# Rows in token order and stores on SyncE, in a retention and MLP kernel

## The chip, the cores and the metric

One core of one Trainium2 chip. The metric is device time in microseconds (us) of one launch, with all inputs and the output in HBM. Lower is better. Engines are called TensorE (PE in the profile; PEld are its weight loads), VectorE (DVE), ScalarE (ACT), GpSimd (POOL) and SyncE (SP). A name with a q behind it (ACTq, SPq) is that engine's own queue, where it issues DMAs.

## The reference

Retention over 8 batches of 576 tokens, 8 heads of 64, then a low-rank mix over tokens and an MLP over channels with a residual:

```python
def _attn_ref(q, k, v):                       # q, k, v: (8, 8, 576, 64) float32
    scores = scale * np.matmul(q, k.transpose(0, 1, 3, 2))
    gamma = 1.0 - 2.0 ** (-5.0 - np.arange(H))
    Dmat = np.where(rel >= 0, gamma[:, None, None] ** rel[None, :, :], 0.0)
    return np.matmul(scores * Dmat[None], v)

def _moe_ref(x, U, V, w_ch1, w_ch2):          # x: (8, 576, 512), U: (576, 32), V: (32, 576)
    xt = x.transpose(0, 2, 1)
    h = xt @ U @ V
    u = x + h.transpose(0, 2, 1)
    ch = np.maximum(u @ w_ch1, 0.0) @ w_ch2   # w_ch1: (512, 2048), w_ch2: (2048, 512)
    return u + ch
```

## The kernel before

A batch has four chunks of 128 tokens and 64 tokens left over; two batches share a ninth chunk, number `XC`. Each batch has a front (loads, casts, transposes, retention, mix) and two matmul stages of the MLP, which are called Y1 (relu of u times w1) and Y2 (times w2, plus u). The fronts of later batches are spread by estimated cost between the MLP steps of earlier ones, so the order of emission is the order in which each engine works.

The queries are loaded four tokens to a partition, which gives runs of 1 KB. The rows of q are then permuted within the four chunks, the permutation goes through the whole batch, and the store undoes it:

```python
SKEW, FILL1 = 0.65, (0.33, 0.85)
LOAD2, FRONT2 = (0.75, 0.12), 0.15
STQ = nc.scalar                                   # stores are issued on ACT
osb_pool = tc.tile_pool(name="osb_pool", bufs=3)
...
def load_q(g):                                    # one load, 1 KB runs
    nc.sync.dma_start(out=f, in_=q[g, :, t0:t0 + 4 * P, :].rearrange("h (p j) d -> p h j d", j=J))
...
def Y2(self, i, f0, nf=4):                        # last step of a chunk
    ...
    o_sb = osb_pool.tile([P, dm], FP32, tag="o_sb", name="o_sb")
    nc.vector.tensor_tensor(out=o_sb, in0=self.ps[i], in1=self.st["u", c], op=ALU.add)
    dst = out_flat[row0:row0 + P, :]
    if c != XC:
        dst = dst.rearrange("(p j) d -> j p d", j=J)
    stores.append(lambda: STQ.dma_start(out=dst, in_=o_sb))
    if len(stores) > 1:
        stores.pop(0)()                           # issued one chunk late
```

The loads of q, k, v and x and the transposes of six batches are issued on SyncE, the weights of the MLP on GpSimd.

## Time and profile before

| | before |
|---|---|
| median of 3 runs | 371.43 us (370.94 to 376.23) |
| profiled span | 371.7 us |
| TensorE busy | 332.2 us |
| front, to the first matmul of Y1 | 31.2 us |
| Y1 of batch 0 | 28.5 us |
| after the last matmul | 7.7 us |

The prediction shows the lines by stage and the places where TensorE stands still. One view that it lacks is that of ACT's waits. The lines give the instruction that waits, what it waited for, us in total, how many times, and the longest.

```profile
ACT y_4028 L703 <- DMA out_dram<-o_sb: 10.3, 1, 10.3
ACT s_sb L470 <- DMA out_dram<-o_sb: 7.4, 3, 4.7
...
ACT uT L388 <- DMA kT<-kv: 4.4, 1, 4.4
...
ACT y_2209 L703 <- DMA kv_f<-in_v_dram: 3.0, 1, 3.0
```

The relus (`y`) and copies (`uT`, `s_sb`) of ACT read PSUM, not a DMA's tile. 25 us of ACT's idle time end with a DMA all the same, because a store ahead of them in ACT's queue waits for one. The last two of these lines are the holes that the prediction is about; behind the 10.3 us TensorE does not stand still.

### The profile page before, as it was taken

The numbers are of one execution on the slowest core, as the hardware profiler recorded it, in microseconds if no ns is written. First come the engines' busy times: TensorE is split into PE (matmuls) and PEld (weight loads), VectorE is DVE, ScalarE is ACT, GpSimd is POOL, SyncE is SP. The second block draws the span as 40 slices with busy tenths as digits, with TensorE's granted clock in tenths as the row PEclk, the third lists the DMA queues.
The fourth block names the chain that finished last, engine by engine and source line by source line (L and its number), as shares of the span: only waits on it lengthen the run. The fifth ranks groups of instructions, "written<-read, shape, count | busy, mean of one in ns | idle before, by whom it ended". The sixth has DMA issues, their size and how long they took to land.

```text
span 371.7 us, 6390 instructions
## 1 busy us (share of the span) xinstructions
PE 332.2 (89%) x2606; PEld 184.4 (50%) x2642; DVE 154.8 (42%) x245; ACT 146.2 (39%) x284; POOL 56.2 (15%) x81
## 2 busy tenths in 40 slices
PE   3778687898997999996999999998999999999991
PEld 1454244445663554444665554545765544467540
DVE  5672546652853661463412662264424532210020
ACT  3425453135553126512574135504662156148200
POOL 8640620310130111112112001201100000000000
PEclk9989969999999999999899999999999999999997
DMA  8999899939999999988994347999902200110112
GB/s 208 194 200 243 175 176 266 203 83 180 192 173 222 167 118 178 212 131 168 159 212 91 78 110 157 218 112 159 112 15 67 56 23 0 50 65 2 56 48 64
DMA packets 127149, 49.66 MB, mean 134 GB/s; under 512 B 110192, under 2 KB 122480, under 8 KB 127120
## 3 DMA queue, kind: packets, MB, share of 16 engines
q1 hardware_dynamic: 117440, 35.48, 58.9%
q10 hardware_dynamic: 5456, 9.59, 9.1%
q0 software_dynamic: 4224, 4.19, 7.1%
q8 instruction: 20, 0.33, 0.5%
q14 instruction: 9, 0.07, 0.1%
HBM read 36.92 MB, written 9.44 MB: 125 GB/s over the span
## 4 chain that ended last, share of the span: by engine, by line
PE 67%; DMA 13%; SPq 7%; DVE 6%; ACT 3%; issue 2%; ACTq 0%; POOL 0%; DVEq 0%; POOLq 0%
DMA kv_f<-in_v_dram 5%; DMA kT<-kv 4%; PE psc L487 3%; SPq L313 3%; PE po L535 2%; DVE q_bf L299 2%; PE pu L600 2%; PE ph L581 2%; DMA q_f<-in_q_dram 2%; PE pss L465 2%; DVE ret L523 2%; SPq L401 2%; SPq L340 1%; PE psa L564 1%; DMA x_f<-in_v_dram 1%
## 5 line engine op out<-in xcount | busy, mean ns | idle before, releaser
L699 PEld LDWEIGHTS <-w_sb 128*128 128x128 bf16 x768 | 73.0, 99 | 52.7 <-issue 7.4
L303 POOL TENSOR_TENSOR kv<-kv_f,vscale 128x512 bf16<-128x512 f32 x32 | 34.3, 1071 | 190.4 <-DMA kv_f<-in_v_dram 133.6
L523 DVE TENSOR_TENSOR ret<-psc,tri 128x1024 bf16<-128x1024 f32 x32 | 39.1, 1223 | 33.0 <-PE psc L487 32.9
L470 ACT ACTIVATE s_sb<-pss 128x512 bf16<-128x512 f32 x32 | 19.1, 596 | 61.1 <-PE pss L465 36.1
L587 DVE TENSOR_TENSOR ut<-ph,xt 128x512 bf16<-128x512 f32 x36 | 24.4, 688 | 44.8 <-PE ph L581 44.8
L543 DVE TENSOR_TENSOR xt<-po,qscale 128x512 bf16<-128x512 f32 (+1 forms) x37 | 25.5, 689 | 21.1 <-PE po L535 20.9
L388 ACT ACTIVATE uT<-pu 128x512 bf16<-128x512 bf16 x32 | 18.9, 596 | 25.8 <-PE pu L600 21.3
L535 PEld LDWEIGHTS <-ret 128*128 128x128 bf16 x288 | 12.7, 100 | 10.5 <-DVE ret L523 5.9
L331 DVE CAST kv<-kv_f 128x512 bf16<-128x512 f32 x32 | 14.6, 462 | 4.2 <-DMA kv_f<-in_k_dram 4.1
L487 PE MATMUL psc<-qT,kT 64*128 64x128 bf16 x256 | 13.4, 227 | 2.9 <-DMA kT<-kv 1.7
L487 PEld LDWEIGHTS <-kT 64*128 64x128 bf16 x256 | 7.6, 97 | 15.5 <-issue 11.2
L600 PEld LDWEIGHTS <-ut 128*128 128x128 bf16 x128 | 9.6, 98 | 11.1 <-issue 3.2
L600 PE MATMUL pu<-ident,ut 128*128 128x128 bf16 x128 | 12.4, 219 | 3.0 <-ACT uT L388 2.6
L535 PE MATMUL po<-kv,ret 128*128 128x64 bf16 x256 | 13.2, 196 | 1.7 <-DVE ret L523 1.4
L299 DVE CAST q_bf<-q_f 128x512 bf16<-128x512 f32 x30 | 13.4, 509 | 3.0 <-DMA q_f<-in_q_dram 3.0
L709 PEld LDWEIGHTS <-y_4028 128*128 128x128 bf16 x80 | 7.8, 98 | 9.3
L465 PE MATMUL pss<-kv 128*128 128x128 bf16 x112 | 11.5, 229 | 0.8 <-ACT s_sb L470 0.7
L465 PEld LDWEIGHTS <-kv 128*128 128x128 bf16 x112 | 8.8, 102 | 5.9 <-issue 1.0
L410 PE MATMUL psq<-ident,q_bf 128*128 128x128 bf16 x32 | 4.1, 308 | 7.7 <-DVE q_bf L299 7.6
L709 PEld LDWEIGHTS <-y_1084 128*128 128x128 bf16 x80 | 7.2, 98 | 6.7
L709 PEld LDWEIGHTS <-y_3202 128*128 128x128 bf16 x80 | 7.2, 98 | 6.6
L709 PEld LDWEIGHTS <-y_2209 128*128 128x128 bf16 x80 | 7.2, 98 | 6.6
(585 smaller groups left out, 590.4 us busy)
## 6 DMA issues: line engine op xcount, KB each, us to landing
out_dram<-o_sb ACTq DMA_DIRECT2D x36, 256.0 KB
q_f<-in_q_dram SPq DMA_DIRECT2D x8, 1024.0 KB
kv_f<-in_k_dram SPq DMA_DIRECT2D x32, 256.0 KB
kv_f<-in_v_dram SPq DMA_DIRECT2D x32, 256.0 KB
w_sb<-in_moe_w_ch_dram POOLq DMA_DIRECT2D x8, 512.0 KB, 8.3
x_f<-in_k_dram SPq DMA_DIRECT2D x8, 128.0 KB
x_f<-in_q_dram SPq DMA_DIRECT2D x8, 128.0 KB
x_f<-in_v_dram SPq DMA_DIRECT2D x8, 128.0 KB
```

The costliest lines, as they stand in the source:

```text
L299: nc.vector.tensor_copy(out=dst, in_=src)
L303: nc.gpsimd.tensor_tensor(out=dst[rows], in0=src[rows], in1=vscale[rows, c, :, None].to_broadcast([n, H, D]), op=ALU.mult,)
L465: nc.tensor.matmul(pss[:, hp, :], pair_cols(st["k", c], hp), pair_cols(vt, hp), start=(first and hp == 0), stop=True, skip_group_check=True,)
L470: nc.scalar.activation(out=s_sb, in_=pss, func=AF.Copy)
L487: nc.tensor.matmul(psc[0:n, hl, hp, 0:n], kT[pb:pb + HALF, hp, 0:n], qTv[pb:pb + HALF, hp, 0:n], start=True, stop=True,)
L523: nc.vector.tensor_tensor(out=ret[0:n].rearrange("p (hp hl) i -> p hl hp i", hl=2)[:, :, :, 0:n], in0=psc[0:n, :, :, 0:n], in1=mask[0:n, N ...
L535: nc.tensor.matmul(po[0:n, hl, hp * D:(hp + 1) * D], ret[:, h, 0:n], vt[:, h, :], start=((c == 0 or not cross) and hp == 0), stop=True, sk ...
L543: nc.vector.tensor_tensor(out=st["x", c][rows].rearrange("p (hp hl d) -> p hl hp d", hl=2, d=D), in0=po[rows, :, 0:NHP * D].rearrange("p h ...
L587: nc.vector.tensor_tensor(out=ut, in0=ph, in1=st["x", c], op=ALU.add)
L600: nc.tensor.transpose(pu[:, cc, :], self.st["u", c][:, cc * P:(cc + 1) * P], ident)
L699: nc.tensor.matmul(ps[:, 0:n], w1_sb[:, cc, f * P:(f + 1) * P], uT[:, cc, t0:t0 + n], start=(cc == 0), stop=(cc == NCC - 1),)
L709: nc.tensor.matmul(self.ps[i], self.y1[:, f, i * P:(i + 1) * P], w2_sb[:, f, :], start=(f == 0), stop=(f == NF - 1),)
```

## The change

The intent is to have each store as one transfer of 128 natural rows, to take the stores out of ACT's queue, and to shorten the first two stages. For batches 0 and 1 q keeps its 1 KB runs, and q^T is put back in order as it leaves PSUM; the other six batches load q in natural rows of 256 B. The masks, scales and the mixer's weights need no permuted copies any more. The order of the second stage is new too.

```diff
-    SKEW = 0.65
-    FILL1 = (0.33, 0.85)
-    LOAD2 = (0.75, 0.12)
-    FRONT2 = 0.15
+    SKEW = 0.7
+    FILL1 = (0.2, 0.8)
+    LOAD2 = 0.62
+    CAST2 = (0.85, 0.3)
+    FRONT2 = 0.3
-    STQ = nc.scalar
+    STQ = nc.sync
... (one table of positions instead of two, mixer weights copied without a permutation, parts of the first casts on ACT)
     def load_q(g):
+        if g < 2:
+            return nc.sync.dma_start(... "h (p j) d -> p h j d" ...)
+        for m in range(4):
+            i = nc.sync.dma_start(
+                out=f[:, m * dm:(m + 1) * dm].rearrange("p (h d) -> p h d", d=D),
+                in_=q[g, :, t0 + m * P:t0 + (m + 1) * P, :].rearrange("h s d -> s h d"),
+            )
... (TQ)
                 self.copy(
-                    qT[:, :, h0:h0 + 2].rearrange("p m hp (j i) -> p m (hp j) i", j=J),
-                    ps.rearrange("p hp j (m i) -> p m (hp j) i", m=4),
+                    qT[:, :, hp].rearrange("p m (i j) -> p m i j", j=J),
+                    ps.rearrange("p j (m i) -> p m i j", m=4),
... (Y2)
-            if c != XC:
-                dst = dst.rearrange("(p j) d -> j p d", j=J)
... (second stage: q(1) is cast ahead of k and x, the mixer's copies come first)
-        lo2 = [(0, f) for f, in loads_of(2)]
-        spread(lo2, at(0, LOAD2[0]), at(1, LOAD2[1]))
+        def load_2():                       # all loads of batch 2 in one block
+            i = load_q(2)
+            tc.add_manual_dep(i.ins, w2_part.ins.name, SYNC)
+            for m in range(4):
+                load_kv(2, m)
+            load_x(1)
+        events.append((at(0, LOAD2), load_2))
+        spread([(0, f) for f in cast_2], at(0, CAST2[0]), at(1, CAST2[1]))
```

More of the change, by code (lines that the diff above doesn't have):

```diff
@@ L73 @@
     J = 4
-    PJ = P // J
     XC = 4
@@ L116 @@
     ident = consts.tile([P, P], BF16, name="ident")
-    perm = consts.tile([P, P], BF16, name="perm")
     tri = consts.tile([P, P], BF16, name="tri")
     trix = consts.tile([P, P], BF16, name="trix")
-    posk = consts.tile([P, NCH, H], FP32, name="posk")
-    posq = consts.tile([P, NCH, H], FP32, name="posq")
+    pos = consts.tile([P, NCH, H], FP32, name="pos")
     qscale = consts.tile([P, NCH, H], FP32, name="qscale")
@@ L150, in early_consts @@
         make_identity(nc, ident)
-        nc.vector.tensor_copy(
-            out=perm.rearrange("t (j p) -> t j p", j=J),
-            in_=ident.rearrange("t (p j) -> t j p", j=J),
-        )
         nc.gpsimd.memset(lnb, math.log(scale))
-        for t in (posk, posq):
-            iota(t[:, XC, :], [[0, H]], 4 * P, 1)
-            iota(t[HALF:P, XC, :], [[0, H]], -HALF, 1)
-        iota(posk[:, 0:4, :], [[P, 4], [0, H]], 0, 1)
-        iota(posk[:, 5:9, :], [[P, 4], [0, H]], 0, 1)
-        for j in range(J):
-            r = slice(j * PJ, (j + 1) * PJ)
-            iota(posq[r, 0:4, :], [[P, 4], [0, H]], j, J)
-            iota(posq[r, 5:9, :], [[P, 4], [0, H]], j, J)
-        nc.gpsimd.memset(tri, 0.0)
-        triv = tri.rearrange("p (j i) -> p j i", j=J)
-        nc.gpsimd.affine_select(
-            out=triv, in_=triv, compare_op=ALU.is_gt, fill=1.0, base=0,
-            pattern=[[-1, J], [-J, PJ]], channel_multiplier=1,
-        )
+        iota(pos[:, XC, :], [[0, H]], 4 * P, 1)
+        iota(pos[HALF:P, XC, :], [[0, H]], -HALF, 1)
+        iota(pos[:, 0:4, :], [[P, 4], [0, H]], 0, 1)
+        iota(pos[:, 5:9, :], [[P, 4], [0, H]], 0, 1)
+        make_upper_triangular(nc, tri, val=1.0, diag=True)
         make_upper_triangular(nc, trix, val=1.0, diag=True)
         nc.gpsimd.memset(trix[0:HALF, HALF:P], 0.0)
-        for t in (posk, posq):
-            nc.vector.tensor_tensor(
-                out=t, in0=t, in1=lngs[:, None, :].to_broadcast([P, NCH, H]),
-                op=ALU.mult,
-            )
-        nc.scalar.activation(out=vscale, in_=posk, func=AF.Exp, bias=lnb, scale=-1.0)
-        nc.scalar.activation(out=qscale, in_=posq, func=AF.Exp, bias=0.0, scale=1.0)
+        nc.vector.tensor_tensor(
+            out=pos, in0=pos, in1=lngs[:, None, :].to_broadcast([P, NCH, H]), op=ALU.mult
+        )
+        nc.scalar.activation(out=vscale, in_=pos, func=AF.Exp, bias=lnb, scale=-1.0)
+        nc.scalar.activation(out=qscale, in_=pos, func=AF.Exp, bias=0.0, scale=1.0)
     def clear_a():
@@ L212, in load_mixer @@
             dma.dma_start(out=U_fB[HALF:P, 0, :], in_=moe_U[0:HALF, :])
-    def put_v(t, c0, t0):
-        nc.vector.tensor_copy(
-            out=t[0:R, c0:c0 + 4 * P].rearrange("r (m j p) -> r m j p", j=J, p=PJ),
-            in_=V_nat[:, t0:t0 + 4 * P].rearrange("r (m p j) -> r m j p", j=J, p=PJ),
-        )
-    def put_u(par):
-        f, t, m0 = ((U_fA, U_A, 0), (U_fB, U_B, 1))[par]
-        un = mix_pool.tile([P, 4, R], BF16, tag="un", name="un")
-        nc.vector.tensor_copy(out=un, in_=f[:, m0:m0 + 4, :])
-        ps = big("psu")
-        nc.tensor.matmul(
-            ps[:, 0:4 * R], perm, un.rearrange("p m r -> p (m r)"), start=True, stop=True
-        )
-        nc.vector.tensor_copy(
-            out=t[:, m0:m0 + 4, 0:R],
-            in_=ps[:, 0:4 * R].rearrange("p (m r) -> p m r", r=R),
-        )
     def put_mixer_a():
-        put_u(0)
+        nc.vector.tensor_copy(out=U_A[:, 0:4, 0:R], in_=U_fA[:, 0:4])
         nc.vector.tensor_copy(out=U_A[0:HALF, 4, 0:R], in_=U_fA[0:HALF, 4, :])
-        put_v(V_A, 0, 0)
+        nc.vector.tensor_copy(out=V_A[0:R, 0:S], in_=V_nat)
     def put_mixer_b():
-        put_u(1)
-        nc.vector.tensor_copy(out=V_A[0:R, 4 * P:S], in_=V_nat[:, 4 * P:S])
+        nc.vector.tensor_copy(out=U_B[:, 1:5, 0:R], in_=U_fB[:, 1:5])
         nc.vector.tensor_copy(out=U_B[HALF:P, 0, 0:R], in_=U_fB[HALF:P, 0, :])
-        put_v(V_B, P, HALF)
-        nc.vector.tensor_copy(out=V_B[0:R, HALF:P], in_=V_nat[:, 0:HALF])
+        nc.vector.tensor_copy(out=V_B[0:R, HALF:5 * P], in_=V_nat)
     def v_rows(par, i):
@@ L280, in load_q, with cast_q @@
         t0 = HALF * par
-        f = stage.tile([P, H, J, D], FP32, tag="q_f", name="q_f", bufs=1)
-        i = nc.sync.dma_start(
-            out=f, in_=q[g, :, t0:t0 + 4 * P, :].rearrange("h (p j) d -> p h j d", j=J)
-        )
-        t = q_pool.tile([P, NHP, J, 2, D], BF16, tag="q_bf", name="q_bf")
-        sts[p]["q", par] = t
-        sts[p]["q_f", par] = f
-        return i
-    def cast_q(g, hps=range(NHP), quick=False):
+        f = stage.tile([P, 4 * dm], FP32, tag="q_f", name="q_f", bufs=1)
+        t = q_pool.tile([P, 4 * dm], BF16, tag="q_bf", name="q_bf")
+        sts[p]["q_f", par], sts[p]["q", par] = f, t
+        if g < 2:
+            return nc.sync.dma_start(
+                out=f.rearrange("p (h j d) -> p h j d", j=J, d=D),
+                in_=q[g, :, t0:t0 + 4 * P, :].rearrange("h (p j) d -> p h j d", j=J),
+            )
+        first = None
+        for m in range(4):
+            i = nc.sync.dma_start(
+                out=f[:, m * dm:(m + 1) * dm].rearrange("p (h d) -> p h d", d=D),
+                in_=q[g, :, t0 + m * P:t0 + (m + 1) * P, :].rearrange("h s d -> s h d"),
+            )
+            first = first or i
+        return first
+    def cast_q(g, parts=range(4), quick=False):
         st = sts[g // 2]
         f, t = st["q_f", g % 2], st["q", g % 2]
-        for hp in hps:
-            dst = t[:, hp]
-            src = f[:, 2 * hp:2 * hp + 2].rearrange("p hl j d -> p j hl d")
-            if quick and hp > 1:
+        for i in parts:
+            dst, src = t[:, i * dm:(i + 1) * dm], f[:, i * dm:(i + 1) * dm]
+            if g < 2:
+                dst = dst.rearrange("p (j hl d) -> p j hl d", j=J, d=D)
+                src = src.rearrange("p (hl j d) -> p j hl d", j=J, d=D)
+            if quick and i > 1:
                 nc.scalar.activation(out=dst, in_=src, func=AF.Copy)
@@ L316, in load_kv, with cast_kv @@
         sts[p]["kv_f", m + 5 * par] = f
-    def cast_kv(g, m):
+    def cast_kv(g, m, quick=False):
         cast_v(g, m)
-        cast_k(g, m)
+        cast_k(g, m, quick)
     def cast_v(g, m):
@@ L327, in cast_v, with cast_k @@
         sts[p]["k", c], sts[p]["v", c] = t[:, 0], t[:, 1]
-    def cast_k(g, m):
+    def cast_k(g, m, quick=False):
         st, c = sts[g // 2], m + 5 * (g % 2)
-        nc.vector.tensor_copy(out=st["k", c], in_=st["kv_f", c][:, 0])
+        if quick:
+            nc.scalar.activation(out=st["k", c], in_=st["kv_f", c][:, 0], func=AF.Copy)
+        else:
+            nc.vector.tensor_copy(out=st["k", c], in_=st["kv_f", c][:, 0])
     def load_x(p, part=None):
@@ L369, in cast_xqk @@
         f, rows = sts[p]["x_f"], x_rows(part)
-        nc.vector.tensor_copy(out=sts[p]["x3"][rows, 0:2], in_=f[rows, 0:2])
+        dst, src = sts[p]["x3"][rows, 0:2], f[rows, 0:2]
+        if part == 0:
+            nc.scalar.activation(out=dst, in_=src, func=AF.Copy)
+        else:
+            nc.vector.tensor_copy(out=dst, in_=src)
     def pair_cols(t, hp):
@@ L401, in TQ @@
                 nc.sync.dma_start_transpose(
-                    out=qT[:, m].rearrange("p hp (j i) -> p (hp j) i", j=J),
-                    in_=t[m * PJ:(m + 1) * PJ].rearrange("p hp j hl d -> p (hp j hl d)"),
+                    out=qT[:, m], in_=t[:, m * dm:(m + 1) * dm]
                 )
                 return
-            for h0 in range(0, NHP, 2):
-                ps = big("psq", BF16, [P, 2, J, P])
-                for hp in range(2):
-                    for j in range(J):
-                        nc.tensor.transpose(
-                            ps[:, hp, j, :],
-                            t[:, h0 + hp, j].rearrange("p hl d -> p (hl d)"), ident,
-                        )
+            for hp in range(NHP):
+                ps = big("psq", BF16, [P, J, P])
+                for j in range(J):
+                    c0 = (hp * J + j) * P
+                    nc.tensor.transpose(ps[:, j, :], t[:, c0:c0 + P], ident)
                 self.copy(
-                    qT[:, :, h0:h0 + 2].rearrange("p m hp (j i) -> p m (hp j) i", j=J),
-                    ps.rearrange("p hp j (m i) -> p m (hp j) i", m=4),
-                    act=not (self.quick and h0),
+                    qT[:, :, hp].rearrange("p m (i j) -> p m i j", j=J),
+                    ps.rearrange("p j (m i) -> p m i j", m=4),
+                    act=not (self.quick and hp % 2),
                 )
@@ L451, in TX @@
                 self.copy(xT[:, 1, :, 0:n], ps[:, 1, :, 0:n])
-                self.copy(xT[:, 0, :, 0:n], ps[:, 0, :, 0:n], act=False)
+                self.copy(xT[:, 0, :, 0:n], ps[:, 0, :, 0:n])
             else:
@@ L765, in first_front @@
         fr.TK(0)
-        cast_kv(0, 1)
+        cast_kv(0, 1, True)
         fr.SC(0)
+        put_mixer_a()
         fr.ST(0)
@@ L771, in first_front @@
         fr.RV(0)
-        cast_kv(0, 2)
+        cast_kv(0, 2, True)
         fr.SC(1)
@@ L777, in first_front @@
         fr.RV(1)
-        put_mixer_a()
         w1a = load_w1(range(0, 2))
@@ L782, in first_front @@
         fr.ST(2)
+        cast_kv(0, 3, True)
+        load_w1(range(2, 4))
         fr.MA(0)
+        fr.TX(HALF)
         warm(WARM[3])
-        fr.TX(HALF)
         fr.RV(2)
         fr.MA(1)
-        cast_kv(0, 3)
-        load_w1(range(2, 4))
         fr.SC(XC, HALF, None)
-        warm(WARM[4])
         fr.TK(3)
         fr.MA(2)
+        fr.SC(3, cross=None)
         fr.ST(3)
-        fr.SC(3, cross=None)
         fr.CR(XC, HALF)
@@ L883 @@
                 w2_part = load_w2()
-        fill = [(0, put_mixer_b)] + [(216, lambda c=c: first.MH(c)) for c in range(2)]
-        fill += [(0, lambda: cast_k(1, 0)), (0, lambda: cast_xqk(0, 1))]
+        fill = [(216, lambda c=c: first.MH(c)) for c in range(2)]
         fill += [(0, lambda: cast_q(1, (0, 1))), (0, lambda: cast_q(1, (2, 3)))]
         fill += [(216, lambda c=c: first.MH(c)) for c in range(2, 4)]
+        fill += [(0, lambda: cast_k(1, 0)), (0, lambda: cast_xqk(0, 1))]
         casts = [(cast_k, 1, m) for m in range(1, 4)]
@@ L912, in at @@
             return starts[g] + share * (starts[g + 1] - starts[g])
+        events.append((at(0, 0.05), put_mixer_b))
         spread(fill, at(0, FILL1[0]), at(0, FILL1[1]))
-        lo2 = [(0, f) for f, in loads_of(2)]
-        def first_load(f=lo2[0][1]):
-            tc.add_manual_dep(f().ins, w2_part.ins.name, SYNC)
-        lo2[0] = (0, first_load)
-        spread(lo2, at(0, LOAD2[0]), at(1, LOAD2[1]))
+        def load_2():
[5 more added lines that the diff above has]
+        events.append((at(0, LOAD2), load_2))
+        cast_2 = [lambda hp=hp: cast_q(2, (hp,)) for hp in range(NHP)]
+        cast_2 += [lambda m=m: cast_kv(2, m) for m in range(4)] + [lambda: cast_x(1)]
+        spread([(0, f) for f in cast_2], at(0, CAST2[0]), at(1, CAST2[1]))
         lo = at(1, FRONT2)
```

## The prediction

> **What bounds the kernel now.** I read the page's first two parts, then busy time by stage in windows that I chose by what TensorE runs, then the places where TensorE or the engine that feeds it stands still. The stages (columns: window in us and its length; busy us and counts of PE, weight loads, DVE, ACT, POOL; granted clock; DMA share; GB/s):
>
> ```profile
> PE 332.2 (89%) x2606; PEld 184.4 (50%) x2642; DVE 154.8 (42%) x245; ACT 146.2 (39%) x284; POOL 56.2 (15%) x81
> ...
> 0.00:31.20 31.20, 19.61 (x205) 11.91 (x208) 18.75 (x40) 10.17 (x18) 17.77 (x42) 0.95 1.17 212
> 31.20:59.70 28.50, 21.22 (x123) 10.31 (x125) 12.51 (x21) 14.17 (x24) 8.43 (x9) 0.88 1.03 197
> 59.70:165.00 105.30, 98.25 (x852) 53.49 (x861) 54.45 (x86) 41.45 (x81) 16.84 (x17) 1.00 1.01 174
> 165.00:180.00 15.00, 11.72 (x94) 7.05 (x92) 5.68 (x8) 3.78 (x9) 3.12 (x3) 0.89 1.05 151
> 180.00:364.10 184.10, 181.37 (x1344) 101.59 (x1360) 62.76 (x92) 76.59 (x156) 9.99 (x10) 1.00 0.50 89
> 364.10:371.70 7.60, 0.00 (x0) 0.00 (x0) 0.68 (x1) 0.00 (x0) 0.00 (x0) 0.70 0.20 64
> ```
>
> From 60 us on this is a TensorE kernel: 98% busy from 180 to 364. What can be won is TensorE's 39.5 idle us (371.7 - 332.2): 11.6 in the first front (0 to 31), 7.3 in the next stage, about 10 in a few holes between 60 and 180, 7.6 after the last matmul. The chain of waits gives PE 67%, DMA 13% and the queue of SyncE 7%.
>
> The holes. TensorE's timeline at three places (start, length, what; in brackets the idle us before it and what ended it):
>
> ```profile
> 43.95 0.38 PE L581 MATMUL ph<-a_sb,V_A 128*128 128x512 bf16 x1 [1.60 <-DVE ut L587]
> ...
> 47.25 1.46 PE L410 MATMUL psq<-ident,q_bf 128*128 128x128 bf16 x12 [2.33 <-DVE q_bf L299]
> ...
> 92.58 0.40 PE L487 MATMUL psc<-qT,kT 64*128 64x128 bf16 x8 [1.73 <-DMA kT<-kv]
> ...
> 175.34 0.70 PE L699 MATMUL ps_y_2228<-uT,w_sb 128*128 128x320 bf16 x4 [3.22 <-ACT y_2209 L703]
> ```
>
> ACT's timeline ahead of two holes:
>
> ```profile
> 118.81 1.67 ACT L388 ACTIVATE uT<-pu 128x512 bf16<-128x512 bf16 x3 [4.40 <-DMA kT<-kv]
> ...
> 174.26 0.55 ACTq L724 DMA_DIRECT2D out_dram<-o_sb  x1
> 174.85 0.44 ACT L703 ACTIVATE y_2209<-ps_y_2210 128x320 bf16<-128x320 f32 x1 [3.04 <-DMA kv_f<-in_v_dram]
> ```
>
> The last of all engines' timelines: the last addition on DVE starts at 364.09 and the span ends at 371.7.
>
> ```profile
> 357.90 7.45 ACTq L724 DMA_DIRECT2D out_dram<-o_sb  x3
> ...
> 364.09 0.69 DVE L717 TENSOR_TENSOR o_sb<-ps_y_4301,ut 128x512 f32<-128x512 f32 x1 [2.76 <-PE ps_y_4301 L709]
> ```
>
> The reader is to see that ACT's 3.04 us at 172 and 4.40 us before 118.8 end with a DMA that has nothing to do with its own operand: just ahead stands a store in ACT's queue. In the built program each plain DMA waits for an earlier DMA that used the same one of eight semaphores, so a store on ACT waits for a load or transpose of SyncE, and the relus behind it wait too.
>
> **What the Trainium skill says.** (1) "DMA: Bandwidth & Descriptors", section "Why a DMA increments its semaphore by 16 and not by 1": the number of DMA engines is the largest number up to 16 that divides the slowest dimension of both sides. The stores of permuted rows go out as 4 x 32 x 512, so to 4 engines; those of the shared chunk as 128 x 512, so to 16. The trace agrees (same columns as the stages):
>
> ```profile
> 351.50:352.50 1.00, 1.00 (x7) 0.44 (x5) 0.00 (x0) 0.00 (x0) 0.00 (x0) 1.00 0.73 283
> 358.00:359.50 1.50, 1.50 (x8) 0.69 (x7) 0.00 (x0) 0.00 (x0) 0.00 (x0) 1.00 0.26 100
> 366.20:370.30 4.10, 0.00 (x0) 0.00 (x0) 0.00 (x0) 0.00 (x0) 0.00 (x0) 0.61 0.24 74
> 83.00:84.50 1.50, 1.50 (x9) 0.75 (x8) 0.26 (x1) 0.00 (x0) 0.00 (x0) 1.00 1.01 329
> 40.00:44.00 4.00, 2.35 (x12) 1.06 (x12) 2.81 (x7) 1.79 (x3) 2.08 (x3) 1.00 1.05 229
> ```
>
> A permuted store alone holds the DMA share at 0.24 to 0.26, four sixteenths; the shared chunk's store in the first row reaches 0.73 and 283 GB/s. (2) Same page, section "Why small descriptors are slow (HBM only)": a 256 B descriptor carries a fixed overhead. The last two rows agree: q alone in 1 KB runs 329 GB/s, k and v in 256 B runs 229. (3) "TensorE: Matmul & The Clock Gate", Part 1: after about 3.4 us idle TensorE runs at half clock for a window. The trace grants 0.81 of the clock from 40 to 50 us and 0.83 from 170 to 180, after the idle stretches above: such a hole is paid about one and a half times.
>
> **The change, part by part.**
>
> *Stores.* All become 128 x 512, 16 engines, on SyncE. At the end the last 256 KB take 4.1 us on the wire (third row of that fence); at 283 GB/s they take 0.9. Gain at the end 3 us, all on the path. In the middle ACT no longer queues behind loads: TensorE's holes of 2.18 us (before 119.5), 3.22 (before 175.3) and 1.17 (before 255.9) go, and 1.7 us of half clock (one window of 3.4 us) after the second: 8.3 us. Transposes crawl where they share four engines with a store: from 84 to 92 us four transposes and two stores hold the DMA share at 1.41 and the first kT lands at 92.54, which is the 1.73 us hole above. Gain 1.5.
>
> *Order of the second stage.* DVE works there in order: mixer parts of batch 1, `ut`, k, x, then q. In the changed order the mixer parts come at 0.05 of the first MLP instead of 0.33, q ahead of k and x, and the whole block starts at 0.2. The q of batch 1 lands at 33.7 us and is cast only from 45.93. That removes most of 1.60 + 0.22 + 2.33 + 0.57 us idle and about 2.5 us of half clock (6.8 us of it from 46 to 53, partly idle anyway). I take 5.5, since x lands only at 39.5 and kv at 41 to 46 and something else will be waited for.
>
> *First front.* Three casts of k and one of x go from DVE to ACT (0.4 to 1.2 us each in DVE's row), the permuting matmul with its 1.02 us hole and two warming matmuls go, ten iotas less on POOL; q^T leaves PSUM in four pieces (about 0.6 each, two on ACT, two on DVE) instead of two of 1.02 and 0.69. DVE is 6.8 of 10 us busy from 10 to 20, in series with TensorE. I take 2.5 us. A check on both: w2's four blocks land at 50.5, 53.7, 56.2 and 59.5 us, and w1 gates q(1) as before. The second matmul stage, which starts at 59.7 now, can't start ahead of 50.5; gaining 8 us keeps it behind.
>
> *q loads of six batches.* 1 MB in 256 B rows: at 229 instead of 329 GB/s, 4.6 instead of 3.2 us, 1.4 us more for each, 8 us in all of DMA time, and 3 more issues each on SyncE (about 0.6 us, longer when queues are full). From 200 to 215 us the DMA share is 0.3, and loads are emitted two steps (some 10 us) ahead of their casts, so I put this beside other work. The 32-partition transposes of q become the form that k has; TensorE's matmuls of those batches are unchanged.
>
> *New waits.* Stores on SyncE wait for DVE, and loads and transposes stand behind them. A store is issued one chunk late, so its o_sb is done some 3.5 us before. SKEW 0.7 and FRONT2 0.3 move fronts closer to the MLP that needs them. I allow 3 us.
>
> Sum: 371.4 - 3 - 8.3 - 1.5 - 5.5 - 2.5 + 3 = 353.6. TensorE's work stays near 330, so this leaves 24 us idle, of which 9 in the first front and 4.5 after the last matmul.
>
> **Rivals.** *SyncE becomes the bound:* its queue carries 36 stores and 18 loads more, and the chain already has 7% of it. For: transposes take about 1.2 us each to issue even when idle, and a wait for o_sb holds all loads. Against: 8 transposes of 1.2 us, some 15 loads of 0.55 to 0.65 and 4 to 5 stores of 0.4 sum to some 21 us of the 39.5 that a batch takes in the steady stretch. It would eat 10 us: about 363. *The early stage is bound by DMA, not order:* share 1.17 and 1.03 in the first two stages; then starting fill early only moves TensorE's wait to x, kv or w2, and the second stage gives 2 instead of 5.5, the front 1: about 359. *Everything bought back by 256 B rows*: the 8 us land in full on the path, about 362; against it the low share after 200 us. *Better:* if no new wait appears, 350.
>
> **Range and chances.** The stores' gains are read off holes that the change removes by construction (13 us); the order's 8 are softer. With all soft gains lost and 3 us of new waits it is 362; with all kept and none new 350, and some small holes could go as well. So 354 us, 346 to 362. The 2% line is 364.0: faster 0.89, same 0.09, slower 0.02.
>
> **What would show it.** Right: last DVE addition to end of span about 4 us instead of 7; ACT never idle on a DMA; no TensorE hole over 2 us after 60 us; clock 1.0 at 170 to 180; q cast of batch 1 before 42 us and w2's stage starting at 51 to 53; DMA share never near 0.25 with a store alone. Wrong: SyncE's queue in the chain well over 7% with waits on o_sb, TensorE waiting for qT, kT or w2, or the first MLP starting no sooner than 31 us.

## The result

The changed kernel takes 361.04 us (median of 4 runs, 360.50 to 361.89), the kernel before 373.33 us on the same chip in the same rounds (370.94 to 376.23). The ratio is 0.967, with a 95% interval of 0.958 to 0.976: faster, inside the predicted range, 7 us above the predicted time. A ratio is the mean time of one kernel's fast runs over that of the other's of the same rounds, so it isn't quite the ratio of the medians. The kernel before scatters from 367.7 to 377.7 us.

From the page of the changed kernel: busy time, two DMA queues (packets, MB, share of 16 engines) and the chain of waits by engine.

```profile
PE 330.6 (92%) x2638; PEld 182.9 (51%) x2638; DVE 151.6 (42%) x235; ACT 149.8 (42%) x292; POOL 53.0 (15%) x71
...
q1 hardware_dynamic: 141344, 44.92, 66.5%
...
q10 hardware_dynamic: 656, 0.15, 0.2%
...
PE 62%; DMA 18%; SPq 12%; DVE 3%; issue 2%; POOL 1%; ACT 0%; DVEq 0%
```

TensorE's work is what it was; its idle time fell from 39.5 to 28.1 us. The stores' 9.4 MB are in SyncE's queue (q1) now. ACT is gone from the chain, and SyncE's queue has 12% of it where it had 7%.

Busy time by stage, in windows cut as those of before (the fourth lies the same way around the start of batch 3's Y1); columns as in the prediction.

```profile
0.00:27.90 27.90, 18.01 (x203) 11.31 (x204) 15.15 (x33) 13.11 (x24) 14.56 (x32) 1.00 1.18 197
27.90:51.30 23.40, 20.87 (x173) 10.62 (x173) 13.79 (x22) 16.05 (x29) 8.22 (x9) 1.00 1.02 196
51.30:159.70 108.40, 97.95 (x792) 52.72 (x793) 51.28 (x80) 39.28 (x76) 17.14 (x17) 0.98 1.09 191
159.70:174.70 15.00, 15.00 (x161) 9.72 (x158) 8.85 (x12) 7.13 (x17) 3.13 (x3) 1.00 0.92 171
174.70:354.90 180.20, 178.77 (x1320) 98.57 (x1317) 61.85 (x89) 74.21 (x149) 10.00 (x10) 1.00 0.43 89
354.90:358.70 3.80, 0.02 (x1) 0.00 (x0) 0.69 (x1) 0.00 (x0) 0.00 (x0) 1.00 0.18 69
```

The first two stages are 8.5 us shorter, the fourth window has no idle time where it had 3.3 us at 0.89 of the clock, and the tail is half as long. The third window is 3.1 us longer: 10.4 us idle instead of 7.0. There lies the missing part. TensorE's timeline, in it and at its start:

```profile
51.27 0.39 PE L681 MATMUL ps_y<-w_sb,y 128*128 128x512 bf16 x1 [1.55 <-DMA w_sb<-in_moe_w_ch_dram]
...
80.68 10.80 PE L671 MATMUL ps_y<-uT,w_sb 128*128 128x320 bf16 x68 [3.86 <-DVE o_sb L689]
102.70 0.29 PE L482 MATMUL po<-s_sb,qT 64*128 64x64 bf16 x8 [1.50 <-DVE xt L515]
107.29 0.29 PE L482 MATMUL po<-s_sb,qTx 64*128 64x64 bf16 x8 [1.68 <-DVE qTx L476]
```

TensorE waits 3.86 us for a PSUM bank that DVE's addition `o_sb` has to read first. DVE's timeline there, and at the end:

```profile
79.94 0.69 DVE L689 TENSOR_TENSOR o_sb<-ps_y,ut 128x512 f32<-128x512 f32 x1 [4.42 <-DMA out_dram<-o_sb]
...
101.62 0.43 DVE L303 CAST kv<-kv_f 128x512 bf16<-128x512 f32 x1 [2.12 <-DMA kv_f<-in_k_dram]
106.08 0.43 DVE L303 CAST kv<-kv_f 128x512 bf16<-128x512 f32 x1 [2.30 <-DMA kv_f<-in_k_dram]
...
354.96 0.69 DVE L689 TENSOR_TENSOR o_sb<-ps_y,ut 128x512 f32<-128x512 f32 x1 [2.76 <-PE ps_y L681]
```

The addition itself waits for a store: the pool has three `o_sb` buffers, this is batch 0's fourth chunk, and no store had landed (the first lands at 79.82 us). SyncE's queue says why:

```profile
55.14 6.14 SPq L250 DMA_DIRECT2D q_f<-in_q_dram  x4
61.39 1.00 SPq L282 DMA_DIRECT2D kv_f<-in_k_dram  x1
...
74.32 1.31 SPq L312 DMA_DIRECT2D x_f<-in_v_dram  x2
75.73 1.54 SPq L694 DMA_DIRECT2D out_dram<-o_sb  x3
81.39 3.02 SPq L250 DMA_DIRECT2D q_f<-in_q_dram  x4
```

From 55 to 75.6 us the queue issues the 18 loads of batch 2, of which the first waits for a part of w2. The first three stores stand behind that block and go out together at 75.73. The next loads, those of batch 3, start at 81.39; the casts at 101.62 and 106.08 wait for k of batch 3, DVE works in order, and TensorE has its holes of 1.50 and 1.68 us.

By stage (us, first matmul to first matmul, from the two traces):

| stretch | before | after | difference |
|---|---|---|---|
| front | 31.18 | 27.93 | -3.25 |
| Y1, batch 0 | 28.54 | 23.34 | -5.20 |
| Y2, batch 0 | 24.53 | 23.58 | -0.95 |
| Y1, batch 1 | 25.68 | 29.41 | +3.73 |
| Y2, batch 1 | 24.85 | 26.07 | +1.22 |
| Y1, batch 3 | 26.20 | 21.71 | -4.49 |
| Y1, batch 4 | 17.69 | 18.81 | +1.12 |
| after the last matmul | 7.68 | 3.80 | -3.88 |
| the other ten | 185.4 | 184.1 | -1.29 |
| sum | 371.7 | 358.7 | -13.0 |

### The profile page after: what moved, and what is told of

Read it like the earlier page. It is cut to its first block, busy times and chain, and to the rows that moved or that the text cites. A ratio compares the mean times of both kernels' runs of the same rounds, so it can differ in the third digit from the quotient of the medians.

```text
span 358.7 us, 6423 instructions
## 1 busy us (share of the span) xinstructions
PE 330.6 (92%) x2638; PEld 182.9 (51%) x2638; DVE 151.6 (42%) x235; ACT 149.8 (42%) x292; POOL 53.0 (15%) x71
## 4 chain that ended last, share of the span: by engine, by line
PE 62%; DMA 18%; SPq 12%; DVE 3%; issue 2%; POOL 1%; ACT 0%; DVEq 0%
PE ps_y L681 30%; PE ps_y L671 23%; DMA kv_f<-in_v_dram 6%; SPq L282 6%; DMA w_sb<-in_moe_w_ch_dram 5%; DMA kv_f<-in_k_dram 4%; SPq L312 3%; DMA x_f<-in_q_dram 2%; PE psc L459 2%; SPq L250 2%; PE pu L572 2%; PE ph L553 1%; PE po L507 1%; PE pss L437 1%; PE psa L536 1%
## 5 line engine op out<-in xcount | busy, mean ns | idle before, releaser
L671 PE MATMUL ps_y<-uT,w_sb 128*128 128x320 bf16 (+1 forms) x768 | 141.2, 328 | 4.1 <-DVE o_sb L689 3.9
L681 PE MATMUL ps_y<-w_sb,y 128*128 128x512 bf16 x576 | 141.1, 379 | 3.1 <-DMA w_sb<-in_moe_w_ch_dram 2.3
L675 ACT ACTIVATE y<-ps_y 128x320 bf16<-128x320 f32 (+1 forms) x192 | 94.3, 491 | 81.7 <-PE ps_y L671 72.9
L681 PEld LDWEIGHTS <-y 128*128 128x128 bf16 x576 | 52.9, 98 | 54.2 <-DMA w_sb<-in_moe_w_ch_dram 1.7
L689 DVE TENSOR_TENSOR o_sb<-ps_y,ut 128x512 f32<-128x512 f32 x36 | 24.8, 690 | 72.6 <-PE ps_y L681 68.2
L515 DVE TENSOR_TENSOR xt<-po,qscale 128x512 bf16<-128x512 f32 (+1 forms) x37 | 25.5, 690 | 20.8 <-PE po L507 20.5
L303 DVE CAST kv<-kv_f 128x512 bf16<-128x512 f32 x29 | 15.5, 542 | 9.8 <-DMA kv_f<-in_k_dram 9.1
L268 DVE CAST q_bf<-q_f 128x512 bf16<-128x512 f32 x30 | 12.2, 466 | 3.4 <-DMA q_f<-in_q_dram 3.4
L543 ACT ACTIVATE a_sb<-psa 128x512 bf16<-128x512 f32 x8 | 4.7, 593 | 17.7 <-PE psa L536 17.7
```

Of the source, the lines that this page charges most:

```text
L515: nc.vector.tensor_tensor(out=st["x", c][rows].rearrange("p (hp hl d) -> p hl hp d", hl=2, d=D), in0=po[rows, :, 0:NHP * D].rearrange("p h ...
L671: nc.tensor.matmul(ps[:, 0:n], w1_sb[:, cc, f * P:(f + 1) * P], uT[:, cc, t0:t0 + n], start=(cc == 0), stop=(cc == NCC - 1),)
L675: nc.scalar.activation(out=self.y1[:, f, t0:t0 + n], in_=ps[:, 0:n], func=AF.Relu)
L681: nc.tensor.matmul(self.ps[i], self.y1[:, f, i * P:(i + 1) * P], w2_sb[:, f, :], start=(f == 0), stop=(f == NF - 1),)
```

## The experiments

Twelve kernels in three calls, the first two on one chip, the third on another. "Wrong" means that rows of the output, or of q, lie in another order; the amount of work is the same. Medians in us, ratio to the kernel before:

| kernel | what it is | median | ratio (95%) |
|---|---|---|---|
| before 373.50 | | | |
| a_osb4 | changed kernel, 4 `o_sb` buffers, one tile of constants fewer | 354.31 | 0.949 (0.941 to 0.956) |
| a_act | changed kernel, stores on ACT | 357.83 | 0.959 (0.952 to 0.966) |
| a_4eng | meant as four-engine stores; came out as a repeat | 362.03 | 0.970 (0.963 to 0.976) |
| a_q1k | changed kernel, q in 1 KB runs (wrong) | 355.73 | 0.953 (0.945 to 0.961) |
| before 373.50 | | | |
| a_perm | changed kernel, four-engine stores (wrong) | 398.01 | 1.068 (1.056 to 1.080) |
| a_perm4 | the same rows in four 16-engine stores (wrong) | 374.01 | 1.002 (0.993 to 1.011) |
| b_order | kernel before, new order of the second stage | 369.81 | 0.990 (0.978 to 1.002) |
| a_osb4_q1k | a_osb4 and a_q1k together (wrong) | 350.90 | 0.941 (0.932 to 0.950) |
| before 372.67 | | | |
| b_nat_act | kernel before, natural stores on ACT (wrong) | 360.40 | 0.967 (0.960 to 0.974) |
| b_nat_sp | kernel before, natural stores on SyncE (wrong) | 369.49 | 0.993 (0.987 to 0.999) |
| b_sync | kernel before, its own stores on SyncE | 402.21 | 1.080 (1.071 to 1.088) |
| a_osb4_f15 | a_osb4, fronts of batch 2 begun earlier | 354.98 | 0.954 (0.949 to 0.960) |

A ratio to the kernel before is good to about 0.01, and variants are better compared with each other.

**Theory after the trace:** stores behind a block of loads in one in-order queue, with three buffers, make the new holes. **Rivals:** the 256 B rows bring them (loads are late whatever the queue), or stores on SyncE slow its queue everywhere.

### a_osb4: one more buffer

```diff
-    osb_pool = ctx.enter_context(tc.tile_pool(name="osb_pool", bufs=3))
+    osb_pool = ctx.enter_context(tc.tile_pool(name="osb_pool", bufs=4))
-    qscale = consts.tile([P, NCH, H], FP32, name="qscale")
+    qscale = pos
```

The second part is meant only to make room: the query scales overwrite the positions that they are computed from. The result is correct.

> The changed kernel with four output buffers instead of three (room made by writing the query scales over the positions). Queue theory: the 3.86 us hole of TensorE before 80.7 us is the fourth o_sb waiting for the first store, which stood behind eighteen loads in SyncE's queue; with a fourth buffer the hole and the half-clock window after it go, and the loads of batch 3 come earlier: 353 to 356 us against 361. Rate theory (q in 256 B rows makes loads late): the hole only moves, 359 to 362 us.

Measured: 354.31 us, 7.7 us under a_4eng, which is the changed kernel over again. Y1 of batch 1 fell from 29.41 to 24.22 us. SyncE's queue and TensorE's timeline of a_osb4:

```profile
68.14 1.31 SPq L312 DMA_DIRECT2D x_f<-in_v_dram  x2
69.55 6.69 SPq L694 DMA_DIRECT2D out_dram<-o_sb  x3
76.84 2.95 SPq L250 DMA_DIRECT2D q_f<-in_q_dram  x4
```

```profile
75.21 9.04 PE L671 MATMUL ps_y<-uT,w_sb 128*128 128x320 bf16 x64
...
97.88 0.29 PE L482 MATMUL po<-s_sb,qT 64*128 64x64 bf16 x8 [1.44 <-DVE xt L515]
102.27 0.29 PE L482 MATMUL po<-s_sb,qTx 64*128 64x64 bf16 x8 [1.48 <-DVE qTx L476]
```

The stores still stand behind the loads, and Y1 starts at 75.21 without a hole. The later holes stay nearly as they were, so they aren't a consequence of the 3.86 us hole.

The edit did a second thing, though: the early loads are faster with it. GpSimd's timeline where it issues w2, first in the changed kernel, then in a_osb4:

```profile
45.28 3.04 POOL L227 DMA_DIRECT2D w_sb<-in_moe_w_ch_dram  x4
...
40.53 3.09 POOL L227 DMA_DIRECT2D w_sb<-in_moe_w_ch_dram  x4
```

The loads of k and v that are issued from 6 to 15 us take 3.8 to 4.0 us on average, from issue to landing, in the three kernels with this edit, and 5.3 to 5.7 us in the other eleven. So w2 is issued 4.8 us sooner, the loads of batch 2 begin at 49.63 instead of 55.14 us, and the first store lands at 72.64 us, 3.2 us before the fourth addition. In this trace three buffers would have been enough. Why the loads are faster was not tested. The 7.7 us are what the whole edit is worth, and the share of the buffer stays open. That the wait for a buffer makes the hole rests on the trace of the changed kernel and on the next run.

### a_act: the changed kernel with its stores on ACT

```diff
-    STQ = nc.sync
+    STQ = nc.scalar
```

> The changed kernel with its natural-row stores issued from ACT again. Queue theory: no hole before the second Y1, but ACT stands idle on semaphores of loads and transposes again, with TensorE holes of 1 to 3 us in the odd batches as in the kernel before; about 358 to 364 us in sum, the tail stays near 3.8 us because 16 engines carry the store. If SyncE's queue were all of the gain: near 370 us.

Measured: 357.83 us, 4.2 under a_4eng. Here the loads are as late as in the changed kernel (those of batch 2 begin at 56.06 us), there are three buffers, and only the queue of the stores differs: the first store lands at 73.71 us and the hole at 80.7 us is gone. Y1 of batch 1 takes 24.43 us, 4.5 less than in a_4eng (28.93). A hole of 1.15 us at 225 is gone too; in exchange Y2 of batch 0 took 28.59 instead of 23.58 us, with a hole of 1.99 us behind ACT's `uT` and 6.8 us of half clock. With natural rows, then, ACT was the better place for the stores of this schedule. a_osb4 is faster still, but its loads are faster too.

### a_4eng: a miss

```diff
+            if c != XC:
+                dst = dst.rearrange("(j p) d -> j p d", j=J)
```

> The changed kernel with each store cut as 4 x 32 x 512 (same rows, same result), so that it runs on 4 DMA engines as before. Engine theory: from the last addition on DVE to the end of the span 7 to 8 us instead of 3.8, DMA share 0.25 while a store runs alone, transposes beside stores slow; 365 to 369 us. If the number of engines does not matter: 361 us and a tail of 3.8 us.

The build folded the two dimensions into one of 128, since the rows lie one behind the other (the trace has all 36 stores as 128 x 512), so nothing changed: 362.03 us, and a tail of 3.79 us. It serves as a repeat of the changed kernel.

### a_q1k and a_osb4_q1k: q in 1 KB runs

```diff
-        first = None
-        for m in range(4):
-            i = nc.sync.dma_start(... "h s d -> s h d" ...)   # 256 B rows
+        return nc.sync.dma_start(... "h (p j) d -> p h j d" ...)  # 1 KB runs
```

> The changed kernel with q of batches 2 to 7 loaded in one transfer of 1 KB rows; the result is wrong on purpose (queries in another order), all else is the same. If the 256 B rows are hidden as predicted: within 1.5 us of 361. Rate theory: the holes at 80 to 107 us shrink and 355 to 358 us; at most the 8 us of DMA time that I worked out.

> Four output buffers and q of six batches in 1 KB rows (wrong result on purpose). a_q1k gained 5 us over the changed kernel, a_osb4 gained 7. If the 256 B rows cost only because they stand ahead of the first store: no more than 1 us better than a_osb4, 353 to 355 us. If they cost by themselves: 348 to 350 us.

Measured: 355.73 us for a_q1k, 6.3 under a_4eng; its hole at the start of batch 1's Y1 is 1.45 us. Three q loads fewer in the block let the stores go sooner, so this gain and that of a_osb4 overlap. With a_osb4's edit in place, q in 1 KB runs still gains 3.4 us (350.90 against 354.31, on one chip, 0.008 in the ratio, with intervals that overlap): the holes of 1.44 and 1.48 us vanish and Y1 and Y2 of batch 1 fall to 22.36 and 24.58 us. So q in natural rows has a price of its own in this one stretch, through the loads of batch 3, and the rest of the eight us that the prediction reckoned is hidden. The edit makes the runs longer and also makes one issue of four; no run tells which of the two it is.

### a_perm and a_perm4: permuted stores on SyncE

```diff
+            if c != XC:
+                dst = dst.rearrange("(p j) d -> j p d", j=J)
```

In a_perm4 the same rows go out as four stores of 32 partitions, which by the rule of the Trainium skill that the prediction names use 16 engines each.

> The changed kernel, each store but the shared chunk's written to every fourth row again, as one transfer of 4 x 32 x 512 (rows land in the wrong order on purpose). The form a_4eng was folded to 128 x 512 by the build, so this is the test that it missed. Engine theory: share 0.25 while such a store runs alone, 7 to 8 us from the last addition to the end instead of 3.8, loads and transposes beside stores slower; 365 to 370 us. If neither engines nor rows matter: 361.

> The same wrong rows as a_perm, but each store as four transfers of 32 partitions, so on 16 engines. If the number of engines is the cause: tail 4 to 5 us (four issues instead of one), 361 to 364 us. If writing every fourth row is itself slow: tail of 7 to 8 us as in a_perm.

Measured: 398.01 and 374.01 us, both longer than expected. TensorE's timeline of a_perm:

```profile
81.70 12.12 PE L671 MATMUL ps_y<-uT,w_sb 128*128 128x320 bf16 x68 [5.86 <-DVE o_sb L689]
...
161.87 0.61 PE L572 MATMUL pu<-ident,ut 128*128 128x128 bf16 x4 [10.27 <-DVE ut L559]
...
253.75 0.61 PE L572 MATMUL pu<-ident,ut 128*128 128x128 bf16 x4 [10.36 <-DVE ut L559]
```

A store on four engines costs far more than its own time: DVE's casts of k wait 37.9 us in all for loads, and the holes come in the steady stretch as well. The same rows on 16 engines take 24 us less, so most of it is not the order of the rows in HBM. A transpose beside the stores shows the same: `xT` of the third and fourth pair of batches takes 11.24 and 11.76 us from issue to landing in a_perm, and 3.19 and 3.17 us in a_perm4. The 13 us that a_perm4 lies over the changed kernel go with 132 stores instead of 36 in SyncE's queue; I did not test that part alone, so the order of the rows may have a share in it.

### b_order: the new order of the second stage alone

```diff
-    FILL1 = (0.33, 0.85)
+    FILL1 = (0.2, 0.8)
-        fill = [(0, put_mixer_b)] + [(216, lambda c=c: first.MH(c)) for c in range(2)]
-        fill += [(0, lambda: cast_k(1, 0)), (0, lambda: cast_xqk(0, 1))]
+        fill = [(216, lambda c=c: first.MH(c)) for c in range(2)]
... (k and x after q; put_mixer_b at 0.05 of the first MLP)
```

> The kernel before with the changed order of the second stage alone: mixer parts of batch 1 at 0.05, fill at 0.2 to 0.8, q cast ahead of k and x. If the order is what shortens this stage: from the first matmul of the first Y1 to that of the first Y2 about 23 to 24 us instead of 28.5, the front stays at 31 us; 367 to 369 us if nothing gives it back, 371 to 373 if the holes behind stores on ACT grow by it. Rival (DMA bounds the stage): over 27 us in the stage.

Measured: the whole kernel gained too little to be told from nothing (0.990, 0.978 to 1.002). Its trace is one of a slow run, so its durations are loose. Y1 of batch 0 took 22.30 instead of 28.54 us in it, shorter though the run is slow, so the order does what it was meant to do. Where later holes lie:

```profile
90.79 0.61 PE L487 MATMUL psc<-qT,kT 64*128 64x128 bf16 x8 [4.60 <-DMA kT<-kv]
...
174.11 1.23 PE L699 MATMUL ps_y<-uT,w_sb 128*128 128x320 bf16 x4 [3.64 <-ACT y L703]
```

With four-engine stores still there, the wait for kT at 91 us is longer than before, and the hole behind ACT's store at 174 us stays.

### b_nat_act and b_nat_sp: the two halves of the store's change

```diff
-            if c != XC:
+            if False:
```

b_nat_sp has `STQ = nc.sync` as well. Everything else is the kernel before.

> The kernel before with nothing changed but the rows of the stores: natural 128 x 512, still issued from ACT (the output's rows are then in a wrong order, on purpose). It measures what sixteen engines for a store are worth alone. Theory (the count of engines is most of the store's gain): the tail after the last addition falls from 7.6 to about 3.8 us, the kT hole of 1.73 us goes, and the holes behind ACT's stores shrink, since the loads and transposes that ACT's stores wait for no longer crawl: 366 us, ratio to before 0.98 or lower. Rival (the prediction's split: 4.5 for the count of engines, 8.3 for the queue): ratio 0.988, with the holes before 119.5, 175 and 256 us still there in full.

> The same natural rows, stores issued from SyncE: the store part of the change alone, in the old order and with q in 1 KB runs (rows wrong on purpose). The prediction gives this part 12.8 us: ratio 0.966. If the queue wait of 3.9 us in the changed kernel comes only from the block of 18 loads put whole ahead of the stores, it does not appear here, where the loads of batch 2 are spread over the stage and stores lie between them; then no TensorE hole over 3 us before the second MLP's first stage ends. If stores on SyncE wait for loads in any order of emission, a hole of 3 us or more appears at the start of the second MLP, DVE waiting for o_sb's store, and the ratio is 0.98.

Measured: natural rows alone, still on ACT, give 360.40 us, as much as the whole change. Moving the stores to SyncE from there costs 9.1 us. ACT's waits for DMAs after the first front, in b_nat_act:

```profile
ACT s_sb L470 <- DMA out_dram<-o_sb: 6.6, 3, 3.9
...
ACT uT L388 <- DMA kT<-kv: 4.2, 1, 4.2
```

Of the 25 us of such waits 11 are left. The relus wait for no DMA any more: the holes before 175 and 256 us are gone (Y1 of batch 3 takes 21.16 instead of 26.20 us, that of batch 5 21.16 instead of 22.49), with every store still in ACT's queue. Only the wait of `uT` stays, and TensorE's hole behind it is 1.98 us where it was 2.18. The wait for kT at 90 us fell from 1.73 to 0.62 us, and the tail is 3.96 us.

Why ACT's stores waited so long shows in SyncE's queue. The kernel before:

```profile
160.13 8.05 SPq L439 DMA_TRANSPOSE xT<-x_1881  x1
...
168.86 0.57 SPq L313 DMA_DIRECT2D kv_f<-in_v_dram  x1
```

The same place in b_nat_act:

```profile
151.19 3.16 SPq L439 DMA_TRANSPOSE xT<-x  x1
...
155.02 0.70 SPq L313 DMA_DIRECT2D kv_f<-in_v_dram  x1
```

Beside two four-engine stores, issued at 156.46 and 159.07 us, this transpose takes 8.05 us to issue and lands 10.36 us after its start; beside natural ones it takes 3.16 and 5.34 us. In the kernel before ACT's store at 170.57 us waits for the transpose, and its store at 174.26 us for the load of v behind it, landed at 174.19 us. In b_nat_act both had landed (156.53 and 159.73 us) before the stores came up (161.61 and 167.31 us). The profile gives no landing times for the kernel before. These are the last increments of a DMA's semaphore ahead of the next DMA that uses it; in b_nat_act this way gives the profile's own times for all 188 DMAs. Over all transposes of k after 100 us the mean fell from 5.3 to 3.5 us, over all loads of k and v from 6.6 to 5.1 us.

What SyncE costs shows in its queue. In b_nat_act it begins the loads of batch 2 at 53 us:

```profile
53.40 0.37 SPq L282 DMA_DIRECT2D q_f<-in_q_dram  x1
53.86 0.53 SPq L313 DMA_DIRECT2D kv_f<-in_k_dram  x1
```

In b_nat_sp:

```profile
71.74 0.36 SPq L724 DMA_DIRECT2D out_dram<-o_sb  x1
72.20 0.38 SPq L282 DMA_DIRECT2D q_f<-in_q_dram  x1
...
90.54 1.55 SPq L401 DMA_TRANSPOSE qT<-q_bf  x1
92.19 1.24 SPq L425 DMA_TRANSPOSE kT<-kv  x1
```

and TensorE's timeline of b_nat_sp:

```profile
96.95 0.61 PE L487 MATMUL psc<-qT,kT 64*128 64x128 bf16 x8 [7.78 <-DMA kT<-kv]
```

In the old order the first store is emitted ahead of these loads. On ACT it waits for its `o_sb` and holds up nothing but ACT; on SyncE all loads of batch 2 wait with it, 18.8 us longer, and TensorE has a hole of 7.78 us at their end. Neither of the two theories expected this: the queue bites from the other side. `LOAD2 = 0.62` in the changed kernel fits this: with the loads of batch 2 in one block ahead of the stores its trace has no such hole, and has the one at 80.68 us instead.

### b_sync: permuted stores on SyncE, in the kernel before

```diff
-    STQ = nc.scalar
+    STQ = nc.sync
```

> The kernel before with its permuted-row stores moved to SyncE and nothing else: the queue change without the row change. Theory: a four-engine store on SyncE holds up the loads and transposes of its own queue, as when the changed kernel had permuted stores there (398 us): 390 to 400 us, ratio 1.05 to 1.07, so the change of rows is what makes SyncE usable. Rival: ACT's holes go (8.3 us) and the rest is hidden: 365 us, ratio 0.98.

Measured: 402.21 us, 33 over b_nat_sp. As in a_perm, SyncE is usable for these stores only once they are natural.

### a_osb4_f15: an attempt at a better kernel

```diff
-    CAST2 = (0.85, 0.3)
-    FRONT2 = 0.3
+    CAST2 = (0.75, 0.15)
+    FRONT2 = 0.15
```

> The changed kernel with a fourth o_sb buffer, and the fronts of batch 2 begun earlier (FRONT2 0.15 as before the change, casts of batch 2 ending at 0.15 of the second MLP instead of 0.3), so that two steps are longer there and k and v of batch 3 land ahead of their casts. A correct kernel, tried as the best. Theory (the holes of 1.44 and 1.48 us are late casts of batch 3): both go, 351.5 us, ratio 0.941. Rival (casts of batch 2 become late instead, or stores are in the way): 354 us or more, with a new hole of over 1 us at the start of the second MLP.

Measured: 354.98 us, no gain over a_osb4. TensorE's timeline:

```profile
83.67 0.40 PE L459 MATMUL psc<-qT,kT 64*128 64x128 bf16 x8 [2.27 <-DMA kT<-kv]
...
101.31 0.29 PE L482 MATMUL po<-s_sb,qTx 64*128 64x64 bf16 x8 [1.64 <-DVE qTx L476]
```

One of the two holes is gone, but the front begins before its transposes can be there: they still stand behind the three stores. The best correct kernel is a_osb4, at 354.3 us; a_osb4_f15, on another chip, can't be told from it.

## Why the prediction was right and wrong

It said faster, and 346 to 362 us; that held, though 1 us from the edge. Its time, 354, was 7 us too low, and part of its reasoning was wrong in a way that the sum hid: the largest gain came by another way than the one given, which the change happened to hold as well. To that extent it was right by luck.

| step | predicted | measured |
|---|---|---|
| tail | -3 | -3.88 (trace); -3.7 with the rows alone (b_nat_act); a store at the end lands 2.0 us after its issue instead of 5.8 |
| holes behind ACT's stores | -8.3, by moving to SyncE | -6.4 for those before 175 and 256 us (6.1 predicted), by the rows alone (b_nat_act, still on ACT); -0.2 for the one before 119.5 (2.2 predicted) |
| kT hole | -1.5 | 1.73 to 0.62 us, by the rows alone |
| order of the second stage | -5.5 | -5.20 (trace); -6.2 alone (b_order, a slow run), with no clear gain for the whole |
| first front | -2.5 | -3.25 (trace); 30.0 to 30.4 us in the four b_ kernels and 27.8 to 29.7 with the new front, so rather 2 |
| 256 B rows | 0, beside other work | with the three more issues +6.3 (a_4eng against a_q1k, in part through the wait for a buffer), +3.4 with a_osb4's edit in both |
| new waits | +3 | stretches that became longer add 7.1 us in the trace; the wait for a buffer alone is some 4.5 (a_4eng against a_act, Y1 of batch 1) |

- **The step that failed on size is "I allow 3 us".** Its ground was "a store is issued one chunk late, so its o_sb is done some 3.5 us before". That looks at the store waiting for DVE. The wait that came is the other one, DVE waiting for a store to give back a buffer: three buffers, three stores behind 18 loads. All stretches that became shorter sum to 20.1 us in the trace, against 20.8 predicted; those that became longer sum to 7.1. a_act, where the stores don't stand behind that block, has no such hole. That a_osb4 lands at the predicted 354 is chance, since its loads are faster for a reason that the prediction didn't have.
- **The step that failed on cause is "ACT no longer queues behind loads".** The holes before 175 and 256 us went, in the size predicted, but b_nat_act shows that they go with the stores still on ACT. I read the trace rightly as far as "a store in ACT's queue waits for a DMA", and didn't ask why that DMA was late. While stores are on four engines, transposes and loads beside them are late: `xT` before the 175 us hole lands after 10.36 us, with natural rows after 5.34. a_perm (+37 us over the changed kernel) and b_sync (+33 us over b_nat_sp) show how much hangs on this, and a_perm4, with the same rows as a_perm on 16 engines, that it is the number of engines. What goes on inside the DMA engines meanwhile no view shows. The prediction had this step: "transposes crawl where they share four engines with a store". It used it for the 1.73 us hole alone, and not for ACT's waits.
- **Moving the stores to SyncE gained nothing that the runs can show.** It cost 9.1 us in the old order and 4.2 in the new one (a_4eng against a_act). a_osb4 is 3.5 us better than a_act, but with faster loads. Its edit with stores on ACT was not run, so which queue is better then stays open.
- **The order of the second stage** gave what was predicted in its stage. What it gives to the whole depends on the later stages: with the rows alone (360.40) and everything but the queue (a_act, 357.83) the two lie 2.6 us apart, on different chips, although the front and the second stage are 6.5 us shorter. Y2 of batch 0 takes 4 us of this back.
- **"I put this beside other work"** failed for the q loads only in the MLP of batch 1, where loads of two batches follow each other closely; in the steady stretch after 175 us the kernels with natural rows have no hole over 1.3 us.
- **The rival "SyncE becomes the bound", 363 us,** named the right queue, but not the way. (Of the rivals' times 362, for 256 B rows that land in full on the path, lies nearest to 361.04. Taking these rows back in the changed kernel gave 6.3 of its 8 us, 3.4 on top of a_osb4, so there was more in this rival than the prediction allowed.) SyncE's queue isn't full: in the changed kernel it waits 117.9 us for `o_sb`. It is one unlucky order, at the change from batch 1 to 2.
- **The tests named in the prediction:** the tail, the cast of q(1) in time, w2's stage at 51.27 us, the clock of 1.00 around batch 3, ACT's freedom from DMAs after the first front and the DMA share of a store alone (0.95 from 356.6 to 357.2 us) came as said. "No TensorE hole over 2 us after 60 us" failed with 3.86, and SyncE's queue at 12% of the chain was named as the sign of it.
- **A reading that was off:** the row of 0.73 and 283 GB/s is not the shared chunk's store alone, since the four-engine store before it, issued at 346.88 us, lands only at 352.70. A store at the end lands 2.0 us after its issue in the changed kernel and 5.8 us before, which is a gain of 3.8 us and not of 3.

The Trainium skill bears on this in three places. "DMA: Bandwidth & Descriptors", section "Why a DMA increments its semaphore by 16 and not by 1", says how many engines a transfer gets; the tails agree (7.7 us with the store of permuted rows, 4.8 with the same rows in transfers of 32 partitions, 3.8 to 4.0 with natural rows), and natural rows were worth 12.3 us here (b_nat_act). The same page, section "Issuing engines are not separate DMA queues", says that all issuing engines share the same 16 DMA engines and that issuing from several saves only the time to initiate. For bandwidth no run here speaks against it. For time it is short of what was measured: the same 36 stores on SyncE instead of ACT cost 9.1 us, since SyncE worked through its waits in order here (in b_nat_sp the first store at 71.74 us, the load behind it at 72.20). "TensorE: Matmul & The Clock Gate", Part 1, has the clock at half after about 3.4 us of idle time. The trace agrees for the longest hole: after 3.86 us the granted clock is 0.58 for 3.4 us (80.7 to 84.1), and in a_osb4 neither the hole nor the half clock is there. They are not seen as a lower limit, though: before the change half clock also follows a hole of 3.22 us (175.3) and a stage whose longest hole is 2.33 us (46 to 53).

## What to carry to other kernels

When an engine waits in its queue for a DMA that isn't its own, ask why that DMA is late before moving the waiter; a store spread over few DMA engines can be the reason for both. Before stores join loads in one in-order queue, go through both directions at every change of batch: what a store that waits for its data holds up, and which buffer stays taken while a block of loads stands ahead of it. Undo each half of a combined change separately: here the half that looked like the lesser one carried all of the stores' gain, and the other one was paid for with it. And compare the trace of an experiment with its parent's ahead of the place that it is about: an edit that was to make room for a buffer made the early loads faster.

## What the Trainium skill lacked or had wrong

- "DMA: Bandwidth & Descriptors", section "Issuing engines are not separate DMA queues": it leaves out the wait. Elsewhere the page has a semaphore wait on the issuing sequencer, but not what follows for time. Here a DMA that waited held all that stood behind it on its issuing engine: moving natural stores from ACT to SyncE took 369.49 instead of 360.40 us, with the loads of batch 2 issued at 72.20 instead of 53.40 us.
- The same page, section "Why a DMA increments its semaphore by 16 and not by 1": the number of engines is right, but nothing that I found says what a transfer on four of them does to the others: a transpose beside two such stores lands after 10.36 us instead of 5.34. 256 KB stores on 4 instead of 16 engines cost 12.3 us on ACT (372.67 against 360.40) and 33 to 37 us on SyncE (402.21 against 369.49, 398.01 against 361.04).
- No page that I found has the other side of a store: here an output buffer stayed taken until all that stood ahead of its store in the queue was issued. DVE waited 4.42 us for one behind 18 loads, and Y1 of batch 1 took 28.93 us instead of 24.43 (a_4eng against a_act).
